# One transfer for r and k, routing in pairs of chunks, and another order in a batch's last chunk: an RWKV-attention and mixture-of-experts kernel on one core

## The chip, the cores and the metric

The kernel runs on one NeuronCore of a Trainium2 chip. The metric is device time in microseconds of one execution, as the median of three runs. The engines are named as in the profile: PE (TensorE, matmuls), PEld (its weight loads), DVE (VectorE), ACT (ScalarE), POOL (GpSimd) and SP (SyncE, which here only issues transfers).

## What is computed

Attention comes first: a recurrence with a 48 x 48 state per head, over 4 batches, 8 heads and 768 steps. Its output rows (3072 rows of 384) then go through a mixture of experts with one expert per row:

```
for t in range(S):
    kt, vt, rt = (k[:, :, t], v[:, :, t], r[:, :, t])
    cur = np.einsum('bhd,bhe->bhde', u[None] * kt, vt)
    y[:, :, t] = np.einsum('bhd,bhde->bhe', rt, state + cur)
    state = w[None, :, :, None] * state + np.einsum('bhd,bhe->bhde', kt, vt)
...
logits = x @ w_gate
expert_idx = np.argmax(logits, axis=1)
...
h = np.maximum(np.einsum('ecd,edf->ecf', disp, w1), 0.0)
y = np.einsum('ecf,efd->ecd', h, w2)
...
out[i] = gate_w[i] * y[expert_idx[i], pos[i]]
```

`disp` holds, for each of 8 experts, its rows in order of arrival; `gate_w` is the softmax weight of the chosen expert.

## The kernel before, in words

**Attention.** The 768 steps of a batch are cut into 6 chunks of 128, so the main loop has 24 chunks (`NI`), `i` from 0 to 23; a batch's last chunk is `i % 6 == 5`. Within a chunk the recurrence becomes matmuls. `load` (L474) brings r and k, transposed, into a tile `dm`: 48 features of the even heads on partitions 0 to 47, those of the odd heads on 64 to 111. It does that in two transfers, one for each part; the first six chunks take 64 rows in the first transfer, so that the unused partitions hold something. `load_rows` (L484) brings k and v as rows (`bd`, 128 partitions). SP issues the loads five chunks ahead; six buffers of `dm` and of `bd` rotate.

One turn of the main loop (L618) does these steps, written out in this order, and each engine runs its own part in just this order (the schedule is by hand):

- `scores(i+1)` (L516, PE): r times k within the chunk, into PSUM tile `a`.
- `prep_keys(i+3)` (L505, DVE): multiplies `dm` by powers of the decay, the tile `ft`.
- `product(i+3)` (L488, POOL): r times k elementwise, `P`, for the bonus term.
- `scatters` (L170, POOL): writes finished rows of x into their expert's place in DRAM, one indirect transfer per chunk; one per turn below turn 16, two from there.
- `mix` (L75, PE): one PSUM tile `c` that holds the bonus of chunk i+2 and the expert logits of chunk i-1; `mixed` (L85, ACT) copies it out as `ct`.
- `update(i)` (L529, PE): k times v for the next state; left out in a batch's last chunk.
- `masks(i+1)` (L524, DVE): the masked scores go over the diagonal tile `s`.
- `pull` (L90): PE transposes `ct`, DVE copies the result out as `l` (L93).
- `turn` (L101, PE): four transposes that give chunk i-1's rows of x, `xp`; `keep_rows` (L107, ACT) copies them out later.
- `values1`, `state_of`, `diag` and `values2` (L548, L537, L494, L559): outputs `y` of chunk i from the state and the masked scores, copied to `xs` by ACT (L569).

**Routing.** `GROUPS` (L32) sets how many chunks are routed together. After a group's last chunk, `route` (L124) runs as a generator in three parts: six DVE instructions (best expert, one-hot `oh`, L127 to L140); then an exponential on ACT, the matmuls that count ranks (`rk`, L145 to L148) and the lane sums on POOL (L151), one per chunk; then six more DVE instructions (slot and 1/sum, L159 to L165). The first part runs at the end of the turn that follows the group's last chunk, the second and third in the turn after that.

**Expert weights.** Expert 0's weights are loaded and split into a high and a low half during the attention turns 3 to 23 (`wstream`, L235: ACT casts at L249, DVE subtractions at L250). `xtrans(0, j)` (L286) transposes the first 160 rows of expert 0 in three pieces `tp0_0` to `tp0_2`, and its `split` makes `xh` (ACT, L295) and `xl` (DVE, L296) of each. After the loop come `layer1(0, f)` (L300) for expert 0, the routing of the last chunks, and then all experts in passes of PE-bound matmuls (L308 to L310, L327 to L329).

**Start.** `setup1` (L382) computes the powers of the decay in `ft`, by squaring the decay six times and multiplying, each squaring followed by a product with the block before; then a reciprocal (L395) and the product (L396) that fills the other half.

Of the kernel before, what the change touches and what calls it, by code (L numbers as in the profile page):

```python
# [6 lines left out]
F32 = mybir.dt.float32  # L7
# [24 lines left out]
GROUPS = [(0, 4), (4, 4), (8, 4), (12, 4), (16, 2), (18, 2), (20, 2), (22, 1), (23, 1)]  # L32


def rwkv_moe(nc, tc, dmj, rkv, bdc, wv, wu, uv, wg, w1, w2, out, cap):
# [4 lines left out]
    with ExitStack() as ctx:  # L40
# [175 lines left out]
        with ExitStack() as mc:  # L216
# [69 lines left out]
            def xtrans(k, j):  # L286
                q, m = PASSES[k][2], PASSES[k][4]
                pool, tag, bufs = ((ps1, "a1", 1) if k else (psA, "a0", 2), (ps1, "u", 1), (psA, "a0", 2) if k < 2 else (ps1, "a1", 1))[j]
# [93 lines left out]
            def setup1():  # L382
                wc = sup.tile([128, NP], F32, name="wc")
                nc.vector.tensor_scalar(out=wc, in0=wp, scalar1=0.6, scalar2=1.22, op0=ALU.max, op1=ALU.min)
                sq = [wc]
                for i in range(7):
                    t = w128 if i == 6 else sup.tile([128, NP], F32, name=f"sq{i}")
                    nc.vector.tensor_tensor(out=t, in0=sq[-1], in1=sq[-1], op=ALU.mult)
                    sq.append(t)
                    if i < 6:  # L390
                        m = 1 << i
                        nc.vector.tensor_tensor(out=ft[:, :, 64 + m:64 + 2 * m], in0=ft[:, :, 64:64 + m],
                                                in1=sq[i].unsqueeze(2).broadcast_to([128, NP, m]), op=ALU.mult)
                rc = sup.tile([128, NP], F32, name="rc")
                nc.vector.reciprocal(out=rc, in_=sq[6])  # L395
                nc.vector.tensor_tensor(out=ft[:, :, 0:64], in0=ft[:, :, 64:], in1=rc.unsqueeze(2).broadcast_to([128, NP, 64]), op=ALU.mult)  # L396
# [51 lines left out]
            nc.sync.dma_start(out=wup.rearrange("q a p -> q (a p)"), in_=wu)  # L448
# [4 lines left out]
            nc.vector.memset(ft[:, :, 64:65], 1.0)  # L453
# [20 lines left out]
            def load(i):  # L474
# [3 lines left out]
                n = 64 if i < 6 else D  # L478
                rows = dmj[b, c].rearrange("h d m -> (h d) m")
                nc.sync.dma_start(out=dm[0:n].rearrange("q a p c -> q (a p c)"), in_=rows[0:n])  # L480
                (nc.scalar if i < 2 else nc.sync).dma_start(out=dm[64:64 + D].rearrange("q a p c -> q (a p c)"), in_=rows[D:])
# [98 lines left out]

            load(0)
            nc.scalar.copy(out=wd[:, 0, 0:64], in_=zst)
# [35 lines left out]
            for i in range(NI):  # L618
# [29 lines left out]
                scatters(1 if i < 16 else 2)  # L648
# [3 lines left out]
                each(masks, i + 1)  # L652
                to = place_of(i - 1, sm, rows_of)
# [3 lines left out]
                xp = turn(i - 1, T[i - 1]["xs"], ps1)  # L657
# [3 lines left out]
                if i == NI - 1:  # L661
                    pa.close()
                    psA = mc.enter_context(tc.tile_pool(name="psA", bufs=2, space=PSUM))
# [25 lines left out]
            xtrans(0, 2)()  # L689
# [258 lines left out]
def _layout(r, k, v, w, u, w_gate, w1, w2):  # L948
# [8 lines left out]
    def feats(a, fill):  # L957
# [9 lines left out]
        "dmj": np.stack([rt, kt], 4).reshape(B, NC, 2, D, 2 * NP * C),  # L967
# [25 lines left out]
```

## Time and profile before

| | us |
|---|---|
| median of 3 runs | 397.38 (396.44 to 399.8) |
| the profiled execution, its own time | 397.02 |
| its span, first to last instruction | 395.3 |
| mean granted PE clock over the span | 0.991 of full |

How to read it: the profiled execution took 397.02 us, of which 395.3 are the span of its instructions; the 1.7 us around the span don't depend on what is changed here. The attention loop fills the first 133 us, the passes of the experts the rest. Rows of a timeline give a start, a duration, an engine, a source line, an operation, what is written and read with shapes, how many instructions were merged, and in brackets how long the engine stood idle before them and what ended that.

### The profile page before, as it was taken

How to read it: one execution, taken by the hardware profiler on the slowest of the kernel's cores; microseconds unless marked ns; L12 is line 12 of the kernel's file. 1: busy time of each engine (PE TensorE's matmuls, PEld its weight loads, DVE VectorE, ACT ScalarE, POOL GpSimd, SP SyncE). 2: the span in 40 equal slices, each digit the busy share in tenths (PEclk: the TensorE clock that was granted, in tenths of full speed). 3: DMA queues.
4: the chain of work that ended last, by engine and by line, in shares of the span. 5: the costliest groups of instructions: out<-in, count | busy, mean ns of one | idle time of the engine just before them, and what ended most of it. 6: DMA issues, size and time to landing. Idle time of an engine off the chain costs nothing.

```text
span 395.3 us, 9463 instructions
## 1 busy us (share of the span) xinstructions
PE 375.1 (95%) x3587; PEld 338.4 (86%) x3590; DVE 237.2 (60%) x574; ACT 204.4 (52%) x556; POOL 137.7 (35%) x199
## 2 busy tenths in 40 slices
PE   7999999999989789799999999999999999999993
PEld 3677778777767589799999999999999999999992
DVE  6897889898887466554645645645645645643210
ACT  3668787888578334534624624624624624722301
POOL 6122538585673426601501601601601601201203
PEclk9999999999999899999999999999999999999998
DMA  8999878888722546641634644644644644400102
GB/s 174 260 241 263 219 218 236 259 238 264 200 82 71 175 132 189 203 124 21 209 109 131 177 129 133 176 133 133 183 131 127 185 135 129 144 4 16 44 1 70
DMA packets 20633, 59.93 MB, mean 152 GB/s; under 512 B 4303, under 2 KB 4451, under 8 KB 20577
## 3 DMA queue, kind: packets, MB, share of 16 engines
q1 hardware_dynamic: 14848, 44.12, 40.6%
q0 software_dynamic: 5600, 14.72, 11.5%
q8 instruction: 30, 0.49, 0.6%
q10 hardware_dynamic: 128, 0.39, 0.4%
q14 instruction: 27, 0.21, 0.2%
HBM read 49.98 MB, written 10.03 MB: 152 GB/s over the span
## 4 chain that ended last, share of the span: by engine, by line
PE 74%; issue 12%; ACT 5%; DVE 3%; POOL 2%; DMA 1%; POOLq 1%; another core or an unknown queue 0%; SPq 0%; ACTq 0%; DVEq 0%
PE a L310 8%; PE a L309 8%; PE a L308 8%; PE b L327 7%; PE b L328 7%; PE b L329 7%; PE y L565 6%; PE a L522 6%; PE y L556 3%; PE xp L104 3%; PE c L92 2%; ACT s L503 2%; PE c L82 2%; PE tp L291 2%; PE u L534 2%
## 5 line engine op out<-in xcount | busy, mean ns | idle before, releaser
L335 POOL DMA_INDIRECT out<-yo,ids x32 | 32.3, 1009 | 168.1 <-ACT yo L334 166.2
L308 PE MATMUL a<-xh,ws 128*128 128x416 f32 (+1 forms) x216 | 75.3, 349 | 2.2 <-issue 2.0
L313 ACT ACTIVATE hh<-a 128x416 fp32r<-128x416 f32 (+1 forms) x72 | 35.2, 489 | 74.1 <-PE a L310 69.2
L327 PE MATMUL b<-hh,ws 128*128 128x416 f32 (+2 forms) x216 | 73.4, 340 | 0.0
L309 PE MATMUL a<-xl,ws 128*128 128x416 f32 (+1 forms) x216 | 72.5, 336 | 0.1
L310 PE MATMUL a<-xh,ws 128*128 128x416 f32 (+1 forms) x216 | 72.4, 335 | 0.0
L328 PE MATMUL b<-hl,ws 128*128 128x416 f32 (+2 forms) x216 | 71.7, 332 | 0.3 <-issue 0.3
L329 PE MATMUL b<-hh,ws 128*128 128x416 f32 (+2 forms) x216 | 71.5, 331 | 0.0
L314 DVE SCALAR_TENSOR_TENSOR hl<-a,hh 128x416 fp32r<-128x416 f32 (+1 forms) x72 | 39.8, 553 | 50.8 <-ACT hh L313 38.7
L250 DVE TENSOR_TENSOR ws<-wr,ws 128x384 fp32r<-128x384 f32 (+1 forms) x112 | 67.6, 618 | 2.3 <-ACT ws L249 2.3
L503 ACT ACTIVATE s<-eye,l 128x128 f32<-128x128 f32 x168 | 53.8, 392 | 17.2 <-DVE l L93 16.2
L249 ACT CAST ws<-wr 128x384 fp32r<-128x384 f32 (+1 forms) x112 | 60.0, 558 | 2.2 <-DMA xsd<-xr,slot 2.2
L330 DVE COPY yt<-b 128x416 f32<-128x416 f32 (+2 forms) x27 | 14.6, 542 | 66.7 <-PE b L329 64.3
L492 POOL TENSOR_TENSOR P<-dm 112x512 f32<-112x512 f32 x21 | 27.5, 1312 | 48.7 <-DVE dm L508 20.2
L308 PEld LDWEIGHTS a<-xh,ws 128*128 128x128 f32 x216 | 40.7, 188 | 3.3 <-issue 2.4
L328 PEld LDWEIGHTS b<-hl,ws 128*128 128x128 f32 x216 | 40.8, 189 | 0.8 <-issue 0.5
L309 PEld LDWEIGHTS a<-xl,ws 128*128 128x128 f32 x216 | 40.7, 188 | 0.8 <-DVE xl L296 0.5
L329 PEld LDWEIGHTS b<-hh,ws 128*128 128x128 f32 x216 | 40.6, 188 | 0.4
L327 PEld LDWEIGHTS b<-hh,ws 128*128 128x128 f32 x216 | 40.8, 189 | 0.2
L310 PEld LDWEIGHTS a<-xh,ws 128*128 128x128 f32 x216 | 40.6, 188 | 0.4
L274 POOL DMA_INDIRECT xg<-xsd,pidx x32 | 35.0, 1093 | 15.1 <-issue 7.0
L295 ACT CAST xh<-tp 128x416 fp32r<-128x416 f32 (+1 forms) x27 | 12.6, 480 | 52.3 <-PE tp L291 52.3
(147 smaller groups left out, 569.8 us busy)
## 6 DMA issues: line engine op xcount, KB each, us to landing
wr<-w SPq DMA_DIRECT2D x24, 512.0 KB
wr<-w SPq DMA_DIRECT2D x32, 384.0 KB
bd<-bdc SPq DMA_DIRECT2D x24, 384.0 KB
dm<-dmj SPq DMA_DIRECT2D x40, 192.0 KB
dm<-dmj SPq DMA_DIRECT2D x6, 256.0 KB
xg<-xsd,pidx POOLq DMA_INDIRECT x32
out<-yo,ids POOLq DMA_INDIRECT x32
dm<-dmj ACTq DMA_DIRECT2D x2, 192.0 KB
```

The source lines that it names most:

```text
L249: nc.scalar.copy(out=hi, in_=r)
L250: low.append(lambda: nc.vector.tensor_tensor(out=lo, in0=r, in1=hi.bitcast(F32), op=ALU.subtract))
L274: nc.gpsimd.indirect_dma_start(out=xg[k % 2][:q, i].bitcast(I32), out_offset=None, in_=xsd[:, :], in_offset=bass.IndirectOffsetOnAxis(ap=p ...
L308: nc.tensor.matmul(a, lhsT=wh, rhs=xh[:, d, :n], start=d == 0, stop=False)
L309: nc.tensor.matmul(a, lhsT=wh, rhs=xl[:, d, :n], start=False, stop=False)
L310: nc.tensor.matmul(a, lhsT=wl, rhs=xh[:, d, :n], start=False, stop=d == 2)
L313: nc.scalar.activation(hh[:, f, :n], a, AF.Relu)
L314: nc.vector.scalar_tensor_tensor(out=hl[:, f, :n], in0=a, scalar=0.0, in1=hh[:, f, :n].bitcast(F32), op0=ALU.max, op1=ALU.subtract)
L327: nc.tensor.matmul(o, lhsT=wh, rhs=hh[:, f, :n], start=f == 0, stop=False)
L328: nc.tensor.matmul(o, lhsT=wh, rhs=hl[:, f, :n], start=False, stop=False)
L329: nc.tensor.matmul(o, lhsT=wl, rhs=hh[:, f, :n], start=False, stop=f == 7)
L503: nc.scalar.mul(out=s[:, h, p], in_=eye, mul=bon)
```

## The change

Four edits, made together:

1. `dmj` is padded on the host to 128 rows per chunk, and `load` fetches both halves by one transfer to all 128 partitions (512 KB in place of 192 + 192 KB; in the first six chunks in place of 256 + 192 KB). Chunk 0's is SP's first transfer; the small load of the decay, `wup`, goes to ACT's queue.
2. `setup1` builds the powers by doubling inside one tile `pw`, without the separate squarings; ACT copies the result into the one half of `ft`.
3. `GROUPS` are eleven pairs and two single chunks, in place of four groups of four, three pairs and two singles. `scatters` takes one chunk in every turn.
4. In a batch's last chunk `turn` stands ahead of `pull`. In the loop's last turn, all three `xtrans(0, j)` stand ahead of both, and all three splits are issued together; before, two stood behind them and the third behind the loop.

```diff
-GROUPS = [(0, 4), (4, 4), (8, 4), (12, 4), (16, 2), (18, 2), (20, 2), (22, 1), (23, 1)]
+GROUPS = [(i, 2) for i in range(0, 22, 2)] + [(22, 1), (23, 1)]
...
             def setup1():
-                wc = sup.tile([128, NP], F32, name="wc")
+                pw = sup.tile([128, NP, 65], F32, name="pw")
+                wc = pw[:, :, 1]
+                nc.vector.memset(pw[:, :, 0:1], 1.0)
                 nc.vector.tensor_scalar(out=wc, in0=wp, scalar1=0.6, scalar2=1.22, op0=ALU.max, op1=ALU.min)
-                sq = [wc]
-                for i in range(7):
-                    t = w128 if i == 6 else sup.tile([128, NP], F32, name=f"sq{i}")
-                    nc.vector.tensor_tensor(out=t, in0=sq[-1], in1=sq[-1], op=ALU.mult)
...
+                for m in (1, 2, 4, 8, 16, 32):
+                    nc.vector.tensor_tensor(out=pw[:, :, m + 1:2 * m + 1], in0=pw[:, :, 1:m + 1],
+                                            in1=pw[:, :, m:m + 1].broadcast_to([128, NP, m]), op=ALU.mult)
                 rc = sup.tile([128, NP], F32, name="rc")
...
+                nc.scalar.copy(out=ft[:, :, 64:], in_=pw[:, :, 0:64])
+                nc.vector.reciprocal(out=rc, in_=pw[:, :, 64])
...
-            nc.sync.dma_start(out=wup.rearrange("q a p -> q (a p)"), in_=wu)
+            nc.scalar.dma_start(out=wup.rearrange("q a p -> q (a p)"), in_=wu)
+            nc.sync.dma_start(out=dmb[0].rearrange("q a p c -> q (a p c)"), in_=dmj[0, 0])
...
-                nc.sync.dma_start(out=dm[0:n].rearrange("q a p c -> q (a p c)"), in_=rows[0:n])
-                (nc.scalar if i < 2 else nc.sync).dma_start(out=dm[64:64 + D].rearrange("q a p c -> q (a p c)"), in_=rows[D:])
+                if i:
+                    nc.sync.dma_start(out=dm.rearrange("q a p c -> q (a p c)"), in_=dmj[b, c])
...
-                scatters(1 if i < 16 else 2)
+                scatters(1)
...
                 each(masks, i + 1)
+                if i == NI - 1:
+                    pa.close()
+                    psA = mc.enter_context(tc.tile_pool(name="psA", bufs=2, space=PSUM))
+                    acts = [xtrans(0, j) for j in range(3)]
+                if i % NC == NC - 1:
+                    xp = turn(i - 1, T[i - 1]["xs"], ps1)
                 to = place_of(i - 1, sm, rows_of)
                 pull(c, ct, to)
...
-                xp = turn(i - 1, T[i - 1]["xs"], ps1)
+                if i % NC < NC - 1:
+                    xp = turn(i - 1, T[i - 1]["xs"], ps1)
...
                 if i == NI - 1:
...
-                    acts = [xtrans(0, j) for j in range(2)]
                     take(0)
-                    acts[0]()
-                    acts[1]()
+                    for f in acts:
+                        f()
...
-            xtrans(0, 2)()
```

The edits change what stands where on the engines. On PE, turn 5 (a batch's last chunk), between the mix of chunk 4's `xs` and the values of chunk 5, this stands before:

```order
L82 MATMUL c<-xs_747,wgz 32x128
L92 MATMUL c<-pick,ct 128x16
L104 MATMUL xp_795<-idn,xs_747 128x128 x4
L145 LDWEIGHTS tri
L145 MATMUL rk_801<-oh_760,tri 128x32
```

and this now:

```order
L82 MATMUL c<-xs_757,wgz 32x128
L104 MATMUL xp_804<-idn,xs_757 128x128 x4
L92 MATMUL c<-pick,ct 128x16
L145 LDWEIGHTS tri
L145 MATMUL rk_813<-oh_770,tri 128x16
```

The four transposes of `turn` (L104) stand ahead of the transpose of `pull` (L92), which is the one that waits for ACT's `ct`; the rank matmul behind it covers two chunks (16 columns) in place of four.

On PE in the loop's last turn, from the mix of chunk 22's `xs` to the values of chunk 23, this stands before:

```order
L82 MATMUL c<-xs_2374,wgz 32x128 x4
L92 MATMUL c<-pick,ct 128x16
L104 MATMUL xp_2399<-idn,xs_2374 128x128 x4
L145 LDWEIGHTS tri
...
L148 MATMUL rk_2405<-lane,ones 128x16
L291 MATMUL tp_0_2418<-idn,xg_101 128x128 x2
L291 MATMUL tp_1_2421<-idn,xg_101 128x128 x2
L556 MATMUL y_0_2432<-dm_119,snb_126 64x128 x2
```

and this now (L552 is the line of `values1` in the changed file):

```order
L82 MATMUL c<-xs_2432,wgz 32x128 x4
L291 MATMUL tp_0_2461<-idn,xg_101 128x128 x2
L291 MATMUL tp_1_2464<-idn,xg_101 128x128 x2
L291 MATMUL tp_2_2467<-idn,xg_101 128x128 x2
L104 MATMUL xp_2470<-idn,xs_2432 128x128 x4
L92 MATMUL c<-pick,ct 128x16
L145 LDWEIGHTS tri
...
L148 MATMUL rk_2479<-lane,ones 128x16
L552 MATMUL y_0_2498<-dm_119,snb_126 64x128 x2
```

Ten transposes (six of `xtrans`, four of `turn`) now stand between the mix and the instruction that waits for `ct`, where none stood.

On DVE in turns 2 and 3 (L508, now L504, is `prep_keys`; L544, now L540, the state), this stands before:

```order
L544 SCALAR_TENSOR_TENSOR snb_126<-snb_127,w_137,u 128x48 x4
L508 TENSOR_TENSOR dm_114<-dm_114,ft 112x1024
L526 COPY_PREDICATED s_121<-msk,a_597 128x1024
L93 COPY l_464<-c 128x16
L544 SCALAR_TENSOR_TENSOR snb_127<-snb_126,w_137,u 128x48 x4
L508 TENSOR_TENSOR dm_115<-dm_115,ft 112x1024
```

and this now:

```order
L540 SCALAR_TENSOR_TENSOR snb_126<-snb_127,w_137,u 128x48 x4
L127 TENSOR_REDUCE mx_574<-l_446 128x2
...
L140 TENSOR_TENSOR z_583<-l_446,mx_574 128x16
L504 TENSOR_TENSOR dm_114<-dm_114,ft 112x1024
L522 COPY_PREDICATED s_121<-msk,a_588 128x1024
L93 COPY l_620<-c 128x16
L540 SCALAR_TENSOR_TENSOR snb_127<-snb_126,w_137,u 128x48 x4
L159 TENSOR_TENSOR ps_672<-rk_629,oh_581 128x16
...
L165 RECIPROCAL xr_123<-zs_676 128x2
L504 TENSOR_TENSOR dm_115<-dm_115,ft 112x1024
```

Six instructions of routing stand in each of the two turns where none stood; with pairs, every turn from 2 on carries six.

## Rows read from the trace of the kernel before

**Rows 1.** The page, part 1: busy time, share and instructions by engine.

```profile
PE 375.1 (95%) x3587; PEld 338.4 (86%) x3590; DVE 237.2 (60%) x574; ACT 204.4 (52%) x556; POOL 137.7 (35%) x199
```

**Rows 2.** Busy time by stage: turns 2-5, 6-11, 12-17, 18-22, 23.

```profile
core 0: us, PE busy (x) PEld busy (x) DVE busy (x) ACT busy (x) POOL busy (x), PEclk, DMA share, GB/s
27.56:46.85 19.29, 18.79 (x337) 15.00 (x340) 16.58 (x42) 14.92 (x51) 7.22 (x10) 1.00 0.99 248
46.85:76.08 29.23, 27.98 (x510) 22.35 (x511) 25.21 (x56) 23.43 (x78) 18.96 (x18) 1.00 0.78 231
76.08:105.36 29.28, 28.73 (x515) 22.96 (x517) 27.09 (x66) 23.33 (x79) 18.00 (x21) 1.00 0.86 250
105.36:132.73 27.37, 23.96 (x400) 18.48 (x402) 19.58 (x71) 18.94 (x64) 15.13 (x19) 1.00 0.32 105
132.73:137.86 5.13, 5.04 (x48) 3.79 (x51) 2.87 (x17) 1.92 (x7) 2.16 (x3) 0.69 0.45 142
```

**Rows 3.** Timeline of DVE at the start: decay arrives, `ft`, first and sixth chunk.

```profile
4.07 0.17 DVE L384 TENSOR_SCALAR wc<-wup 128x4 f32<-128x4 f32 x1 [2.34 <-DMA wup<-wu]
...
6.03 0.42 DVE L396 TENSOR_TENSOR ft<-ft,rc 128x256 f32<-128x256 f32 x1
...
6.73 1.23 DVE L508 TENSOR_TENSOR dm<-dm,ft 112x1024 f32<-112x1024 f32 x1 [0.27 <-DMA dm<-dmj]
...
25.46 1.22 DVE L508 TENSOR_TENSOR dm<-dm,ft 112x1024 f32<-112x1024 f32 x1 [0.80 <-DMA dm<-dmj]
```

**Rows 4.** Transfers in two short stretches (columns as in rows 2).

```profile
3.00:7.00 4.00, 4.00 (x12) 1.50 (x11) 2.60 (x17) 0.97 (x4) 2.58 (x42) 1.00 1.05 191
...
61.00:62.00 1.00, 1.00 (x26) 0.79 (x25) 1.00 (x3) 0.30 (x1) 0.85 (x1) 1.00 1.02 390
```

**Rows 5.** Timeline of DVE: third part of `route`, four chunks, then two.

```profile
63.02 0.18 DVE L159 TENSOR_TENSOR ps<-rk,oh 128x32 f32<-128x32 f32 x1
...
64.06 1.22 DVE L508 TENSOR_TENSOR dm<-dm,ft 112x1024 f32<-112x1024 f32 x1
...
112.68 0.16 DVE L159 TENSOR_TENSOR ps<-rk,oh 128x16 f32<-128x16 f32 x1
...
113.66 1.22 DVE L508 TENSOR_TENSOR dm<-dm,ft 112x1024 f32<-112x1024 f32 x1
```

**Rows 6.** Timeline of PE in turn 5.

```profile
40.27 0.42 PE L82 MATMUL c<-xs,wgz 128*32 128x128 f32 x8
41.19 0.40 PE L92 MATMUL c<-pick,ct 128*128 128x16 f32 x2 [0.50 <-ACT ct L87]
41.43 0.64 PE L104 MATMUL xp<-idn,xs 128*128 128x128 f32 x4
...
42.71 1.08 PE L565 MATMUL y<-s,bd 128*48 128x128 f32 x16
```

**Rows 7.** Timeline of POOL and ACT in turns 18 and 19.

```profile
107.21 0.98 POOL L172 DMA_INDIRECT xsd<-xr,slot  x1 [0.30 <-issue]
...
108.69 0.65 ACT L569 COPY xs<-y 128x256 f32<-128x256 f32 x2 [1.28 <-PE a L522]
...
113.23 0.98 POOL L172 DMA_INDIRECT xsd<-xr,slot  x1 [0.30 <-issue]
...
114.72 0.68 ACT L569 COPY xs<-y 128x256 f32<-128x256 f32 x2 [1.27 <-PE a L522]
```

**Rows 8.** PE around turn 23 (timeline), the stage's clock (windows), six transposes (chain).

```profile
131.26 0.39 PE L92 MATMUL c<-pick,ct 128*128 128x16 f32 x2 [1.73 <-ACT ct L87]
...
133.73 1.95 PE L565 MATMUL y<-s,bd 128*48 128x128 f32 x16
...
137.58 0.28 PE L310 MATMUL a<-xh,ws 128*128 128x256 f32 x1
...
133.00:135.00 2.00, 2.00 (x28) 1.65 (x22) 1.79 (x11) 0.16 (x1) 0.00 (x0) 0.50 0.74 209
...
157.90 0.65 PE tp L291 x6
```

More of the change, by code (lines that the diff above doesn't have):

```diff
@@ L287, in xtrans @@
                 q, m = PASSES[k][2], PASSES[k][4]
-                pool, tag, bufs = ((ps1, "a1", 1) if k else (psA, "a0", 2), (ps1, "u", 1), (psA, "a0", 2) if k < 2 else (ps1, "a1", 1))[j]
+                pool, tag, bufs = ((ps1, "a1", 1) if k else (psA, "a0", 2), (ps1, "u", 1) if k else (psA, "a0", 2), ((ps1, "u", 1), (psA, "a0", 2), (ps1, "a1", 1))[min(k, 2)])[j]
                 tp = pool.tile([128, m * q], F32, tag=tag, name=f"tp{k}_{j}", bufs=bufs)
@@ L382, in setup1 @@
             def setup1():
-                wc = sup.tile([128, NP], F32, name="wc")
+                pw = sup.tile([128, NP, 65], F32, name="pw")
+                wc = pw[:, :, 1]
+                nc.vector.memset(pw[:, :, 0:1], 1.0)
                 nc.vector.tensor_scalar(out=wc, in0=wp, scalar1=0.6, scalar2=1.22, op0=ALU.max, op1=ALU.min)
-                sq = [wc]
-                for i in range(7):
-                    t = w128 if i == 6 else sup.tile([128, NP], F32, name=f"sq{i}")
-                    nc.vector.tensor_tensor(out=t, in0=sq[-1], in1=sq[-1], op=ALU.mult)
[L389 to L393, printed above, removed]
+                for m in (1, 2, 4, 8, 16, 32):
+                    nc.vector.tensor_tensor(out=pw[:, :, m + 1:2 * m + 1], in0=pw[:, :, 1:m + 1],
+                                            in1=pw[:, :, m:m + 1].broadcast_to([128, NP, m]), op=ALU.mult)
                 rc = sup.tile([128, NP], F32, name="rc")
-                nc.vector.reciprocal(out=rc, in_=sq[6])
-                nc.vector.tensor_tensor(out=ft[:, :, 0:64], in0=ft[:, :, 64:], in1=rc.unsqueeze(2).broadcast_to([128, NP, 64]), op=ALU.mult)
+                nc.scalar.copy(out=ft[:, :, 64:], in_=pw[:, :, 0:64])
+                nc.vector.reciprocal(out=rc, in_=pw[:, :, 64])
+                nc.vector.tensor_tensor(out=ft[:, :, 0:64], in0=pw[:, :, 0:64], in1=rc.unsqueeze(2).broadcast_to([128, NP, 64]), op=ALU.mult)
+                nc.vector.tensor_tensor(out=w128, in0=pw[:, :, 64], in1=pw[:, :, 64], op=ALU.mult)
                 return wc
@@ L579, in each @@
                     f(i, *a)
+            nc.scalar.copy(out=wd[:, 0, 0:64], in_=zst)
             load(0)
-            nc.scalar.copy(out=wd[:, 0, 0:64], in_=zst)
             load(1)
@@ L661, in rwkv_moe @@
                 if i == NI - 1:
-                    pa.close()
-                    psA = mc.enter_context(tc.tile_pool(name="psA", bufs=2, space=PSUM))
-                    acts = [xtrans(0, j) for j in range(2)]
                     take(0)
-                    acts[0]()
-                    acts[1]()
+                    for f in acts:
+                        f()
                 state_of(i)
@@ L966, in _layout @@
     arrays = {
-        "dmj": np.stack([rt, kt], 4).reshape(B, NC, 2, D, 2 * NP * C),
+        "dmj": np.pad(np.stack([rt, kt], 4), [(0, 0)] * 3 + [(0, 64 - D)] + [(0, 0)] * 3).reshape(B, NC, 128, 2 * NP * C),
         "rkv": np.stack([rows(r), rows(k), rows(v)], 3),
```

3 lines of the change are left out of this document (removed).

## The prediction

> **What bounds the kernel now.** I read the page's busy shares first [rows 1]: PE is busy 95% of the span, DVE 60%, ACT 52%. Such an average hides stages, so the table by stage comes next [rows 2]. The passes of the experts, from 138 us to the end, are PE's and the change leaves them alone; what it can win or lose lies before. From turn 2 on PE is busy nearly throughout: 18.79 of 19.29 us, 27.98 of 29.23, 28.73 of 29.28. But DVE stands close behind it: 16.58, 25.21 and 27.09 us of the same stretches. In turns 18 to 22 neither is full (PE 23.96 and DVE 19.58 of 27.37 us): something there waits. The timeline then shows three kinds of wait: DVE for transfers at the start [rows 3], PE for ACT's `ct` in a batch's last chunk [rows 6] and, much longer, in turn 23 [rows 8], and ACT for PE in turns 18 and 19 [rows 7].
>
> **The start.** DVE gets the decay at 4.07 us, starts the product that fills `ft` at 6.03 and the first chunk's keys at 6.73, the last 0.27 of it waiting for the chunk [rows 3]. From 4.07 to 6.03 stand fifteen instructions in 1.96 us; the new chain has eight up to the same product. The removed squarings ran in between the products, though, while in the new chain each product waits for the one before. Bounds: nothing, or the seven instructions at the mean step of 0.13 us, 0.9 us. I take 0.3, nearer to nothing, since the new chain is all dependent. The copy on ACT lies beside the reciprocal and the product on DVE. The 0.27 us go only if the chunk comes in earlier as well: it is now SP's first transfer, alone but for the small `wup`.
>
> **The loads.** In the stretch 3 to 7 us, when nearly only halves of `dm` move, the 16 transfer engines are busy throughout (share 1.05) and bring 191 GB/s; at 61 to 62 us, with `bd` and weights to 128 partitions, they bring 390 GB/s at the same share [rows 4]. So a chunk's 448 KB cost about 2.4 us of transfer time now (estimated, 0.459 MB by 191) and the 512 KB some 1.35 (0.524 MB by 390). If the new load ran no faster than the mix does in turns 2 to 5, at 248 GB/s and full share [rows 2], it would cost 2.1: from six loads a gain of 1.8 us, and 0.13 MB more in each chunk from then on. Either way chunk 5's wait of 0.80 us at 25.46 [rows 3] should go: -0.8. Nothing after it waits on a load, so the remaining time is not won.
>
> Which of the two rates holds for the new load no row settles, since no r and k goes to 128 partitions there. The Trainium skill (SBUF — State Buffer, Door 1: The DMA port swizzle) says that partitions 0 to 63 reach only eight of the sixteen ports, that two transfers to the two halves hardly add up, and that one to all 128 reaches them all; it gives 196 and 328 GB/s at 1 MiB. The trace agrees in kind, with 191 against 390 GB/s. By the page's figures the load would fall from 2.3 to 1.6 us (an estimate from them), and this term would stay -0.8; by the rate of the mix it could come to nothing (rival 3).
>
> **Routing in pairs.** Each half of a `route` takes about the same on DVE whether it covers four chunks or two: the third part 63.02 to 64.06 us, 1.04, and 112.68 to 113.66, 0.98 [rows 5]. Eight pairs in place of four groups of four make 16 halves at 1.0 in place of 8 at 1.04: +7.7 us on DVE, all of it in turns 2 to 17: four halves for two in turns 2 to 5 (+2), six for two in turns 6 to 11 (+4), six for four in turns 12 to 17 (+1.8). Added to DVE's busy time [rows 2]: 18.6 of 19.29, 29.2 of 29.23, 28.9 of 29.28. So it just fits, and DVE becomes the bound of turns 6 to 17; what stands in a batch's last chunk can't be won there. Bounds: 0 if all fits in DVE's gaps, +7.7 if all lands on the path. DVE's gaps sum to 8.9 us over these stages, so I stay near the lower end: +0.6 in turns 2 to 5 (where the wait for chunk 5, just removed, was one of the gaps), +0.5 in 6 to 11, 0 in 12 to 17. Queued behind the six instructions on DVE is `prep_keys`, which is used two turns later, then `masks` and the copy `l`, for which ACT's diagonals wait; ACT has that slack only while DVE is not late by a whole turn.
>
> **Turn ahead of pull.** In turn 5 PE ends the mix at 40.69 and starts `pull` at 41.19: 0.50 us idle [rows 6]. The four transposes of `turn` (0.64 us, the last of it beside what follows) now fill this gap. -0.5 in turn 5; in turns 11 and 17 DVE is the bound by the sum above, and I count 0 and -0.3.
>
> **Turns 18 and 19.** ACT is idle 1.28 and 1.27 us before it copies `y`, though PE's matmuls for it are over; both end 0.50 us after the second of two scatters in a row ends on POOL (108.19 to 108.69, 114.21 to 114.72) [rows 7]. With one scatter per turn no second one stands there. Whether that is the cause the trace doesn't show: bounds 0 and -2.6. I take the middle, -1.3, since two cases are too few to tell.
>
> **Turn 23.** The mix ends at 129.53; PE then waits 1.73 us for `ct` [rows 8], and after `pull`, `turn`, the ranks and four transposes starts the values shortly before 132.73 [rows 2]. By then its granted clock has fallen from 2.4 to 1.2 GHz (0.50 in 133 to 135 us), so the second half of the values takes 1.95 us in place of 1.08 [rows 8, 6]. The first nine matmuls of `layer1` end at 137.86, with waits for the third split in between. In the new order: 0.65 for six transposes [rows 8] and about 0.5 for `turn` lie in the wait; `pull` (0.39) and the ranks take it from 131.26 to 131.75; the values, 2.95 us from 132.73 to 135.68 now, take some 1.65 by the ratio of 1.08 to 1.95, to 133.4; nine matmuls of `layer1`, at about 0.11 each like the transposes, and some waiting for three splits that now stand together on ACT and DVE, to 135. That is -2.8. If the clock falls all the same, the values and `layer1` cost what they did and only the moved transposes are won: -1.4. If `ct` comes as soon as PE is through, -3.4. I take -2.8: PE now idles 0.6 us there, not 1.73. All behind this point, the routing of the last chunks and through it the first splits of expert 1, moves along with it.
>
> **The sum**, against the profiled execution: -0.3 - 0.8 + 0.6 - 0.5 + 0.5 - 0.3 - 1.3 - 2.8 = -4.9. 397.02 - 4.9 = 392.1 us; the median of the runs lies 0.36 above the profiled one, so 392.5.
>
> **The rivals.**
>
> 1. DVE becomes a real bound (slower). Place: turns 2 to 17, where pairs put six instructions into every turn. Price: all 7.7 us on the path in place of 0.6, with the two gains of turns 5 and 17 lost: -4.9 + 7.1 + 0.8 = +3.0, 400.4 us. It decides once DVE's queue has no idle time left between `snb` and the next `masks`. For it speaks that my sums fill turns 6 to 11 to 29.2 of 29.23 us; against it, that DVE has 8.9 us of gaps in total in turns 2 to 17 and most of what it makes is needed a turn or more later.
> 2. The waits are only moved. The stall of turns 18 and 19 isn't the scatters', and the clock falls in turn 23: -4.9 + 1.3 + 1.4 = -2.2, 395.2 us. For it: no row ties PE to POOL. Against it: the idle time of PE in turn 23 shrinks to a third.
> 3. The load gets no cheaper per byte (the edit doesn't do what it says). At 248 GB/s it still gains 1.8 us over six loads, then adds 0.13 MB per chunk to engines that are busy 0.78 to 0.99 [rows 2]; a chunk then comes late somewhere in turns 5 to 8, and the 0.8 is lost again: 393.3 us. By itself this hardly shows.
> 4. Everything goes: both stalls (-2.6), no cost in turns 2 to 11, `ct` at once in turn 23: -4.9 - 1.3 - 1.1 - 0.6 = -7.9, 389.5 us.
>
> **How the numbers follow.** Forecast 392.5 us, chance 0.47 with rival 3 in it (it lies 0.8 us away); rival 2 has 0.28, rival 4 has 0.13, rival 1 has 0.12. A run of this kernel tells about 1% (3.97 us) from no change: below 393.4 counts as faster, above 401.4 as slower. The forecast's own spread is about 391 to 394, of which some three quarters lie below 393.4: 0.36 and 0.13 from rival 4, and a little of rival 2, give 0.51 for faster. Somewhat under half of rival 1 lies above 401.4: 0.05 for slower. The rest, 0.44, is the same. The range reaches up past rival 2 to the lower part of rival 1 and down to rival 4: 389.5 to 397.5.
>
> **What would show each step.** The start: first keys at about 6.4 us, no wait for a transfer before chunk 5's. The loads: over 300 GB/s in the first 7 us. Routing: DVE busy about 29 us in turns 6 to 11, these turns no longer than 30. Turn 5: no idle PE between L82 and L92. Turns 18 and 19: about 1.3 us shorter each if the scatters were to blame. Turn 23: granted clock 1.00 and the first `layer1` over within 6 us of the mix. I would be wrong in kind if turns 6 to 17 together took over 61 us, or if turn 23 were shorter and the passes of the experts started no earlier.

## The result, and the profile after

On the chip of the first comparison the changed kernel takes 392.9 us (median of 20 runs) and the kernel before 397.4 (20 runs): ratio 0.9898, 95% interval 0.9869 to 0.9927. The forecast was 392.5. Several of the terms behind it came out very differently from the working, and on another chip the change gains nothing (ratio 1.0002 in e5 below). Both facts have the same two causes, which the experiments look for.

The profiled execution took 391.79 us, its span 390.1 (before 397.02 and 395.3). Where the 5.2 us went, stage by stage, counted from the first matmul of `values1` in a turn (0.07 us ahead of the bounds of [rows 2]; a turn's length below is from that point to the next turn's); the last column is worked out from e9 and e5 below, the two kernels on chips where the time before is 387.7 us:

| stage | forecast | first chip | chips of e9, e5 |
|---|---|---|---|
| to turn 2 | -0.3 | +0.36 | +0.48 |
| turns 2 to 5 | -0.7 | -0.93 | -0.44 |
| turns 6 to 11 | +0.5 | +0.52 | +1.32 |
| turns 12 to 17 | -0.3 | +0.68 | +1.12 |
| turn 18 to the end of the mix in turn 23 | -1.3 | +0.19 | -0.06 |
| from there to the end of the first `layer1` | -2.8 | -3.94 | -1.35 |
| the rest | 0 | -2.04 | -0.54 |
| sum | -4.9 | -5.16 | +0.53 |

Busy time and stages of the changed kernel, which answer to [rows 1] and [rows 2]; the last two windows answer to [rows 8] (the clock in turn 23) and [rows 4] (the loads at the start):

```profile
PE 372.8 (96%) x3591; PEld 336.7 (86%) x3594; DVE 243.0 (62%) x616; ACT 204.7 (52%) x565; POOL 138.0 (35%) x199
```

```profile
27.85:46.21 18.36, 18.32 (x336) 14.70 (x335) 17.12 (x52) 14.74 (x52) 9.34 (x11) 1.00 0.80 265
46.21:75.96 29.75, 28.65 (x510) 22.91 (x509) 28.57 (x80) 23.55 (x81) 17.32 (x19) 1.00 0.79 265
75.96:105.92 29.96, 29.61 (x510) 23.08 (x509) 28.66 (x81) 23.52 (x81) 18.20 (x20) 1.00 0.76 251
105.92:131.72 25.80, 23.57 (x399) 18.56 (x398) 18.44 (x66) 19.23 (x66) 12.34 (x17) 1.00 0.33 111
131.72:134.74 3.02, 3.02 (x49) 2.46 (x49) 2.88 (x13) 1.46 (x6) 0.00 (x0) 1.00 0.39 110
133.00:135.00 2.00, 2.00 (x25) 1.43 (x21) 1.86 (x11) 1.12 (x4) 0.00 (x0) 1.00 0.69 211
3.00:7.00 4.00, 4.00 (x13) 1.53 (x12) 1.99 (x10) 0.41 (x1) 1.96 (x33) 1.00 1.03 401
```

The loads run at 401 GB/s where they ran at 191, the clock in turn 23 is 1.00 where it was 0.50, DVE's busy time in turns 6 to 11 has grown by 3.36 us (25.21 to 28.57). The timeline of DVE at the start and at the sixth chunk's keys, against [rows 3]:

```profile
4.73 0.17 DVE L386 TENSOR_SCALAR pw<-wup 128x4 f32<-128x4 f32 x1 [2.99 <-DMA wup<-wu]
...
6.57 0.42 DVE L393 TENSOR_TENSOR ft<-pw,rc 128x256 f32<-128x256 f32 x1
...
7.09 1.22 DVE L504 TENSOR_TENSOR dm<-dm,ft 112x1024 f32<-112x1024 f32 x1
...
24.94 1.22 DVE L504 TENSOR_TENSOR dm<-dm,ft 112x1024 f32<-112x1024 f32 x1
```

From the decay to the product the new chain takes 1.84 us (4.73 to 6.57) where the old one took 1.96, but the decay itself comes 0.66 us later. The wait for chunk 5 is gone. PE in turn 5, against [rows 6]: no idle time stands before L92 any more.

```profile
40.19 0.42 PE L82 MATMUL c<-xs,wgz 128*32 128x128 f32 x8
40.55 0.66 PE L104 MATMUL xp<-idn,xs 128*128 128x128 f32 x4
41.11 0.40 PE L92 MATMUL c<-pick,ct 128*128 128x16 f32 x2
```

In turn 9 a routing instruction that took 0.17 us elsewhere, and in turn 9 of the kernel before, takes 1.47. POOL's zero fill of `xg` starts with it and ends with it; in turn 13 the same pair stands at 82.22 and 82.24. The timeline of POOL and DVE, beside [rows 5]:

```profile
62.22 0.49 POOL L151 TENSOR_TENSOR lane<-lane,oh 128x8 bf16<-128x8 bf16 x2
...
62.64 1.47 DVE L164 TENSOR_SCALAR zs<-zs 128x2 f32<-128x2 f32 x1
62.65 1.43 POOL L687 MEMSET xg<- 128x1600 f32 x1
```

The waits of ACT in turns 18 and 19 [rows 7] are gone, and three others stand where two indirect transfers still follow each other on POOL: the scatters in turn 20, the gather in turn 21, the scatters of turns 22 and 23. Here is the second transfer of each with the copy that waited; each copy starts 0.53 to 0.68 us after the transfer's end:

```profile
116.92 0.97 POOL L172 DMA_INDIRECT xsd<-xr,slot  x1 [0.30 <-issue]
...
118.42 0.65 ACT L565 COPY xs<-y 128x256 f32<-128x256 f32 x2 [1.29 <-PE a L518]
...
122.24 1.00 POOL L274 DMA_INDIRECT xg<-xsd,pidx  x1 [0.30 <-DVE snb L540]
...
123.92 0.65 ACT L565 COPY xs<-y 128x256 f32<-128x256 f32 x2 [0.93 <-PE y L561]
...
127.59 1.00 POOL L172 DMA_INDIRECT xsd<-xr,slot  x1 [0.31 <-issue]
...
129.24 0.65 ACT L565 COPY xs<-y 128x256 f32<-128x256 f32 x2 [2.63 <-PE y L561]
```

PE in turn 23, against [rows 8]: no wait for `ct`, and the second half of the values at 1.08 us in place of 1.95.

```profile
129.66 0.69 PE L82 MATMUL c<-xs,wgz 128*32 128x128 f32 x8 [1.34 <-ACT xs L565]
...
131.43 0.29 PE L92 MATMUL c<-pick,ct 128*128 128x16 f32 x2
...
132.32 1.08 PE L561 MATMUL y<-s,bd 128*48 128x128 f32 x16
```

Behind that, PE waited 2.04 us at one place in the passes of the kernel before, and 0.80 us in two parts (0.61 and 0.19) in the changed one. It waits for `hl`, with which DVE frees a PSUM tile (167.45 + 0.42 us in the kernel before), and `hl` waits for ACT's `hh`. ACT stood idle for 2.76 us before that while gathers followed each other on POOL, though PE had ended all its matmuls at 165.89, 1.14 us before ACT went on. Rows of the timeline of the kernel before:

```profile
166.52 1.07 POOL L274 DMA_INDIRECT xg<-xsd,pidx  x1 [0.30 <-issue]
167.03 0.38 ACT L313 ACTIVATE hh<-a 128x256 fp32r<-128x256 f32 x1 [2.76 <-PE a L310]
...
167.93 0.39 PE L308 MATMUL a<-xh,ws 128*128 128x256 f32 x1 [2.04 <-issue]
```

### The profile page after: what moved, and what is told of

Same layout as the page of the kernel before. It is cut to its first block, busy times and chain, and to the rows that moved or that the text cites. A ratio compares the mean times of both kernels' runs of the same rounds, so it can differ in the third digit from the quotient of the medians.

```text
span 390.1 us, 9456 instructions
## 1 busy us (share of the span) xinstructions
PE 372.8 (96%) x3591; PEld 336.7 (86%) x3594; DVE 243.0 (62%) x616; ACT 204.7 (52%) x565; POOL 138.0 (35%) x199
## 4 chain that ended last, share of the span: by engine, by line
PE 67%; issue 13%; DVE 9%; ACT 6%; POOL 2%; DMA 1%; POOLq 1%; DVEq 0%; ACTq 0%
PE a L310 8%; PE a L308 8%; PE a L309 8%; PE b L327 7%; PE b L328 7%; PE b L329 7%; PE y L561 4%; ACT s L499 4%; PE a L518 3%; PE y L552 2%; PE tp L291 2%; PE xp L104 2%; POOL out L335 2%; PE yp L343 2%; DVE s L522 2%
```

## The experiments

e1 to e4 ran on one chip (the kernel before takes 394.84 us there), e5 to e8 on another (387.75), e9 to e11 on a third (387.72), e12 on a fourth (395.05). Ratios are to the kernel before on the same chip. The changed kernel itself ran only on the chip of the first comparison and on that of e5 to e8, so the times of the other runs have no changed kernel beside them, and their theories are judged by the rows above all. The lengths of turns come from one profile each.

**e1: the third edit undone.**

```diff
-GROUPS = [(i, 2) for i in range(0, 22, 2)] + [(22, 1), (23, 1)]
+GROUPS = [(0, 4), (4, 4), (8, 4), (12, 4), (16, 2), (18, 2), (20, 2), (22, 1), (23, 1)]
...
-                scatters(1)
+                scatters(1 if i < 16 else 2)
```

> The changed kernel with the third edit undone (groups of four again, two scatters per turn from turn 16). Theory A: pairs cost on DVE what the trace after shows (turns 6 to 17 took 59.7 us against 58.5 before), and what pairs win lies in turns 18 and 19, where the second of two scatters in a row on POOL holds up everybody who waits for PE. Then turns 6 to 17 fall to about 58.5 us or less, turns 18 and 19 rise from 4.8 and 4.6 to about 6.1 us each, turns 20 and 21 fall back to 4.9 and 4.5 us, and the time is within 1 us of the changed kernel's, 392 to 393.5 us. Theory B: the stall of turns 18 and 19 comes from something else in the change (loads, order); then both stay below 5 us and the time falls to about 391 us. Theory C: the pairs are free on DVE and win 2.6 us as forecast; then the time rises to about 395.5 us.

Ratio 0.9955 (0.993 to 0.998), 393.1 us. Theory A: turns 18 and 19 take 6.04 and 6.07 us again, turns 6 to 17 58.02 (59.71 in the changed kernel), and the profiled span is 389.7 against 390.1. So pairs win 2.7 us in two turns and lose 1.7 in turns 6 to 17 and 1.6 in turns 20 to 22 (the profiles come from two chips, both with such waits). In turn 18 (timeline) ACT and DVE are let go together, 0.47 and 0.51 us after the end of the second scatter, and both wait for PE, which had finished; L191 reads a matmul that stands ahead of the scores:

```profile
106.23 0.98 POOL L172 DMA_INDIRECT xsd<-xr,slot  x1 [0.30 <-issue]
107.68 0.65 ACT L565 COPY xs<-y 128x256 f32<-128x256 f32 x2 [1.25 <-PE a L518]
107.72 0.16 DVE L191 TENSOR_TENSOR pen<-pos,ct 128x4 f32<-128x4 f32 x1 [1.28 <-PE a L518]
```

**e2: the fourth edit undone.**

```diff
-                if i % NC == NC - 1:
-                    xp = turn(i - 1, T[i - 1]["xs"], ps1)
                 to = place_of(i - 1, sm, rows_of)
                 pull(c, ct, to)
...
-                if i % NC < NC - 1:
-                    xp = turn(i - 1, T[i - 1]["xs"], ps1)
+                xp = turn(i - 1, T[i - 1]["xs"], ps1)
...
-                    acts = [xtrans(0, j) for j in range(3)]
+                    acts = [xtrans(0, j) for j in range(2)]
```

(with the transposes back behind `prep_values`, the third behind the loop, and their PSUM places as before)

> The changed kernel with the fourth edit undone (turn behind pull, transposes of expert 0 where they were). Theory A: this edit carries most of the gain: from the end of the mix in turn 23 to the end of the first layer1 the trace after has 4.46 us where before had 8.33, so about 3.9 us come back, the granted clock falls to 0.50 in turn 23 again, and the time is about 396.5 us. Theory B: the passes of expert 1 wait for weights (2.0 us idle before, 0.8 after), and that wait swallows part of what turn 23 loses: 394 to 395 us. Theory C: the clock stays at 1.00 because the loop before it is arranged otherwise; then some 1.7 us come back, 394.5 us.

Ratio 0.9995 (0.9976 to 1.0015), 394.43 us: of the four runs on this chip the one without any gain. PE waits 1.51 us for `ct` again, but the clock of this stretch stays at 1.00, so theory C's time comes closest; from the mix to the first `layer1` it takes 6.85 us against 4.39 with the edit, 2.46 more. Turn 4, which ends behind `pull` and `turn` of turn 5, takes 4.73 against 4.25: the 0.50 us before L92 are back. Not all of the lost gain need be the edit's: in this profile the first values come 1.46 us later than in the changed kernel (last section), and whether the other executions share that isn't shown. PE's timeline, and a window of the stage (the next, 134 to 137 us, has 1.00 as well):

```profile
131.86 0.40 PE L92 MATMUL c<-pick,ct 128*128 128x16 f32 x2 [1.51 <-ACT ct L87]
```

```profile
131.00:134.00 3.00, 2.14 (x33) 1.79 (x35) 1.71 (x7) 1.43 (x5) 0.43 (x2) 1.00 0.41 149
```

**e3: the first two edits left out** (the kernel before with the diffs of edits 3 and 4 of the change).

> The kernel before with the third and fourth edits alone (two transfers per chunk, old chain of powers). Theory A: the load edit is worth the wait of 0.80 us for chunk 5 and loses 0.36 us at the start, where the decay arrives 0.66 us later: then the first keys start at about 6.7 us, the sixth chunk's wait is back at about 25.5 us, and the time is 0.4 us above the changed kernel's, about 393.3 us. Theory B: with six routing instructions more on DVE in turns 2 to 5 the chunk's wait lies beside them and costs nothing; then the old loads are 0.4 us faster, 392.5 us. Theory C: with pairs the slow loads come late in more turns; then 394.5 us or more.

Ratio 0.9939 (0.9916 to 0.9961), 392.29 us. Theory B: the first keys start at 6.63 us, the sixth chunk's wait is 0.17 us in place of 0.80, with the old loads; turns 2 to 5 take 18.37 us, as in the changed kernel (18.36). DVE's timeline:

```profile
24.74 1.23 DVE L508 TENSOR_TENSOR dm<-dm,ft 112x1024 f32<-112x1024 f32 x1 [0.17 <-DMA dm<-dmj]
```

**e4: the decay first.**

```diff
-            nc.scalar.dma_start(out=wup.rearrange("q a p -> q (a p)"), in_=wu)
+            nc.sync.dma_start(out=wup.rearrange("q a p -> q (a p)"), in_=wu)
```

> The changed kernel with the small load of the decay as SP's first transfer again, ahead of the first chunk. Theory A: the decay came late because a load of 512 KB on another queue was ahead of it; then it arrives at about 4.1 us in place of 4.73, the first keys start at 6.4 to 6.5 us in place of 7.09, and all behind moves by 0.6 us: about 392.3 us. Theory B: what is won at the start is lost at the first wait for a chunk in turns 1 to 5; then the values of turn 6 still start at about 46.2 us and the time stays 392.9 us. Theory C: ACT's queue is what made it late, and the 512 KB load delays it just as much on SP's: no change in the start of the first keys.

Ratio 0.9919 (0.9895 to 0.9943), 391.34 us. Theory A and more: the decay is there at 2.45 us and the first keys start at 5.39. Then DVE waits 1.49 us for the first bonus, so the first values start 0.74 us earlier than in the changed kernel (12.99 against 13.73), and that is kept up to turn 6 (45.46 against 46.21).

DVE's timeline:

```profile
2.45 0.75 DVE L386 TENSOR_SCALAR pw<-wup 128x4 f32<-128x4 f32 x1 [0.71 <-DMA wup<-wu]
...
5.39 1.23 DVE L504 TENSOR_TENSOR dm<-dm,ft 112x1024 f32<-112x1024 f32 x1
...
9.96 0.17 DVE L93 COPY bon<-c 128x16 f32<-128x16 f32 x1 [1.49 <-PE c L92]
```

**e5: the changed kernel again, on another chip.** No edit.

> The changed kernel itself, unaltered, beside the other runs on this chip, so that they can be compared with it and not only with the kernel before. Every theory expects a ratio to the kernel before of 0.987 to 0.993, as measured first.

Ratio 1.0002 (0.9991 to 1.0013), 387.92 us: outside of what every theory expected. Turns 2 to 17 take what they took in the changed kernel on the first chip (78.09 us against 78.07), but turn 20 takes 4.71 us in place of 5.72, turn 21 4.37 in place of 5.54 and turn 22 4.05 in place of 5.08. The scatters stand on POOL just as they did; the copy of turn 20 starts with the second of them, without waiting:

```profile
117.08 0.98 POOL L172 DMA_INDIRECT xsd<-xr,slot  x1 [0.31 <-issue]
```

```profile
117.19 0.62 ACT L565 COPY xs<-y 128x256 f32<-128x256 f32 x2
```

**e6: the fills of `xg` taken off POOL.**

```diff
-                if i in (9, 13):
-                    nc.gpsimd.memset(xg[i == 13], 0.0)
...
+            for t in xg:
+                nc.scalar.copy(out=t, in_=zst[:, 0:1].unsqueeze(2).broadcast_to([128, 4, XW]))
             c = mix(T[0]["P"], None, ps1)
```

> The changed kernel, with the two zero fills of xg taken off POOL (turns 9 and 13) and done by ACT before the loop. Theory A: in turns 9 and 13 of the trace after a DVE instruction of routing (L164) took 1.47 us in place of 0.17 and ended with POOL's fill, because the fill keeps it from running; with the fills gone it takes 0.17 us both times, turn 10 falls from 5.76 to about 5.0 us, turns 14 and 15 from 5.41 and 5.39 to about 5.0 each, and the time by 1.5 us to some 0.985 of the kernel before. Theory B: DVE is the bound in those turns by its own sum of instructions; then L164 is shorter but turns 10, 14 and 15 stay above 5.3 us and the time is the changed kernel's.

Ratio 0.9999 (0.9988 to 1.0010), 387.75 us. The mechanism is theory A's, the time is not: L164 takes 0.17 us, turn 10 falls from 5.80 to 4.49 us, turn 14 from 5.42 to 4.73, turn 15 from 5.36 to 4.87, 2.5 us together; and the fills, put where ACT was needed (2.93 us from 8.71), move the first values from 13.85 to 16.56 us. Timeline of DVE in turn 9:

```profile
65.48 0.17 DVE L164 TENSOR_SCALAR zs<-zs 128x2 f32<-128x2 f32 x1
```

**e7: a fill between two indirect transfers.**

```diff
+            def space():
+                nc.gpsimd.memset(spc, 0.0)
...
                 for i in range(m):
+                    if k == 0 and i:
+                        space()
...
                 each(product, i + 3)
+                if i == NI - 1:
+                    space()
                 scatters(1)
...
+                    space()
                     scatters(NI)
                     gather(0)
```

> The changed kernel, with a fill of 4 KB per partition (some 0.9 us) on POOL between the two indirect transfers that follow each other in turn 20 (scatters), turns 20 to 21 (the gather) and turns 22 to 23 (scatters). Theory A: the second of two indirect transfers in a row holds up those who wait for PE; apart from each other they don't, so ACT's waits before the copy xs in turns 20, 21 and 22 (1.29, 0.93 and about 1.0 us more than the matmuls need) go, these turns fall from 5.72, 5.54 and 5.08 to about 4.7 us each, and the time by 1 to 2.5 us. Theory B: any second transfer within some 3 us of the first does it, whatever stands between; then the waits last until 0.5 us after the end of the second, which is now 0.9 us later, and the turns get longer by up to 0.9 us each. Theory C: the waits have nothing to do with POOL: no change in these turns.

Ratio 1.0013 (1.0003 to 1.0024), 388.28 us, and no answer: on this chip there were no waits to remove. Turns 18 to 22 take 22.58 us against 22.59.

**e8: all scatters in pairs.**

```diff
-                scatters(1)
+                scatters((1 if i > 19 else 2 if i % 2 == 0 else 0))
```

> The changed kernel, with two scatters in a row in every even turn from 4 to 18 and none in the odd ones, in place of one per turn: the same transfers, paired. Theory A: the second of each pair holds up ACT's copy xs until about 0.5 us after its end on POOL, as in turns 18 and 19 of the kernel before; ACT shows a wait of 0.5 to 1.3 us before xs in those eight turns, they get longer by about 1 us each, and the time rises by 4 to 10 us over the changed kernel's. Theory B: the stalls of turns 18 to 22 come from something that only those turns have; then the eight turns stay within 0.2 us each and the time is the changed kernel's.

Ratio 0.9975 (0.9961 to 0.9989), 386.64 us. No pair holds anybody up on this chip either, so it doesn't tell theories A and B apart. It gains by accident: the fills now run 1.5 us ahead of L164 (61.83 against 63.35), which takes 0.17 us in both turns.

**e9: the kernel before, on a chip of the quick kind.** No edit.

> The kernel before, unaltered, for a profile on the chip on which the other two of this call run. The ratio of the change was 0.990 on the first chip and 1.000 on the one of the last four runs, and the profile of the changed kernel there had none of the waits of turns 20 to 22. Theory A: those waits are the chip's; on a chip on which the kernel before takes about 388 us it shows no wait of ACT before xs in turns 18 and 19 beyond the matmuls, these take about 4.7 us each in place of 6.1, the wait for ct in turn 23 is about 0.5 us in place of 1.73, and no idle PE before expert 1's weights; on one on which it takes 394 us or more they are all there. Theory B: the waits are there on every chip in the kernel before, and its time differs by something else.

387.61 us. Theory A, in every number: turns 18 and 19 take 4.81 and 4.65 us, the wait for `ct` in turn 23 is 0.43 us, the clock in the windows from 126.66 to 130.63 is 1.00, and PE's wait of 2.04 us in the passes is gone. So is the wait of 0.80 us for chunk 5, with the old loads. Timelines of POOL and ACT in turn 18, beside [rows 7], of PE in turn 23, beside [rows 8], and of DVE at the sixth chunk, beside [rows 3]:

```profile
105.50 0.99 POOL L172 DMA_INDIRECT xsd<-xr,slot  x1 [0.30 <-issue]
```

```profile
105.62 0.61 ACT L569 COPY xs<-y 128x256 f32<-128x256 f32 x2
```

```profile
125.30 0.39 PE L92 MATMUL c<-pick,ct 128*128 128x16 f32 x2 [0.43 <-ACT ct L87]
```

```profile
24.78 1.23 DVE L508 TENSOR_TENSOR dm<-dm,ft 112x1024 f32<-112x1024 f32 x1
```

The two profiles of this kernel show one thing more. In turn 6 a single scatter runs, and on the first chip it holds ACT up as well: the copy `ct` starts 0.54 us after the matmul that it reads has ended (L82, 49.73 + 0.42), in e9 0.19 us after it (49.24 + 0.42, with the scatter at 49.54). The turn takes 5.03 us there and 4.67 here. Timelines of the kernel before and of e9:

```profile
50.02 1.00 POOL L172 DMA_INDIRECT xsd<-xr,slot  x1 [0.17 <-ACT xr L111]
...
50.69 0.27 ACT L87 COPY ct<-c 128x128 f32<-128x128 f32 x1 [0.73 <-PE u L534]
```

```profile
49.85 0.27 ACT L87 COPY ct<-c 128x128 f32<-128x128 f32 x1 [0.37 <-PE c L82]
```

**e10 and e11: a better version, without and with the fills between transfers.** On top of e4 (e11 adds the lines of e7):

```diff
-                if i in (9, 13):
-                    nc.gpsimd.memset(xg[i == 13], 0.0)
...
                 ct = mixed(c, wk)
+                for t in {1: (xg[0],), 2: (xg[1][:, 0:2],), 3: (xg[1][:, 2:4],)}.get(i, ()):
+                    nc.scalar.copy(out=t, in_=zst[:, 0:1].unsqueeze(2).broadcast_to([128, t.shape[1], XW]))
                 update(i)
```

> The changed kernel with the decay loaded first, and with the zero fills of xg done by ACT in turns 1, 2 and 3, where it waits 2.38, 0.87 and 0.75 us for DVE's l. Theory A: both gains add up, 0.75 us at the start and some 2.5 us in turns 10, 14 and 15, while the fills (1.47 us in all for each xg) lie in ACT's waits: about 3 us less than the changed kernel, 384.8 us on a chip like the last, 389 on one like the first. Theory B: the fills on ACT delay the diagonals in turns 1 to 3, and what is won later is lost there: 1 us or less is left.

> The same with a fill of some 0.9 us on POOL between the indirect transfers that follow each other in turns 20 to 23. Theory A: on a chip where the second of two in a row holds up those who wait for PE it takes 1 to 3 us off the kernel of the run beside it; on one where it doesn't, it changes nothing (within 0.5 us). Theory B: the time between them doesn't matter, and where the waits are there they get longer by the 0.9 us of the fill.

Ratios 0.991 (0.989 to 0.993), 384.03 us, and 0.9906 (0.9887 to 0.9926), 384.04 us. e10 is theory A; e11 came onto a chip without the waits, where both of its theories expect no change. In e10 turns 6 to 17 take 57.21 us, where the kernel before takes 57.29 on the same chip (e9): without the fills, routing in pairs costs no more there than the fourth edit wins. ACT's timeline in turn 1 shows that the fill lies in the wait for `l`, of which 0.97 us are left:

```profile
19.57 1.53 ACT L648 COPY xg<-zst 128x1600 f32<-128x1600 f32 x1
22.06 1.86 ACT L499 ACTIVATE s<-eye,l 128x128 f32<-128x128 f32 x6 [0.97 <-DVE l L93]
```

**e12: spaced and unspaced pairs in one kernel** (e11 without the fill between the scatters of turn 20).

```diff
-                    space()
                     scatters(NI)
                     gather(0)
```

> The kernel of the last run with the fill left out between the two scatters of turn 20 and kept between the two parts of the gather and between the scatters of turns 22 and 23: spaced and unspaced pairs in one profile. On a chip that shows the waits at all (the kernel before at 394 us or more), theory A: ACT waits about 1.3 us before xs in turn 20 (the unspaced pair) and, beyond the matmuls, not at all in turns 21 and 22 (the spaced ones): turns 21 and 22 stay at about 4.4 to 4.7 us, turn 20 takes 5.7. Theory B (the time between doesn't matter): turns 21 and 22 are longer as well, by 1 us or more. On a chip without the waits both theories expect about 0.991 of the kernel before and no wait in any of these turns, and nothing is told apart.

This run came onto a chip with the waits (before 395.05 us). Ratio 0.9794 (0.9731 to 0.9857), 386.33 us (4 runs). Theory A: turn 20 takes 5.66 us, turns 21 and 22 4.49 and 4.05. The timeline of POOL and ACT shows both cases. The copy of turn 20 starts 0.47 us after the end of the second, unspaced scatter (113.06 + 0.97). In turn 21 the second gather runs from 118.61 to 119.62, `y` is ready at 118.87 (L567, 117.79 + 1.08), and the copy starts at 119.00, in the middle of it:

```profile
113.06 0.97 POOL L173 DMA_INDIRECT xsd<-xr,slot  x1 [0.30 <-issue]
114.50 0.65 ACT L571 COPY xs<-y 128x256 f32<-128x256 f32 x2 [1.23 <-PE a L524]
...
117.47 0.96 POOL L273 MEMSET spc<- 128x1024 f32 x1
118.61 1.01 POOL L280 DMA_INDIRECT xg<-xsd,pidx  x1 [0.17 <-issue]
119.00 0.61 ACT L571 COPY xs<-y 128x256 f32<-128x256 f32 x2
```

Turn 21 by itself proves little, since an unspaced pair of gathers doesn't always hold anybody up: in turn 21 of the kernel before, on the first chip, the copy also starts in the second gather (and so in e2, at 124.74 in the one from 124.62):

```profile
124.06 1.01 POOL L274 DMA_INDIRECT xg<-xsd,pidx  x1 [0.30 <-DVE slot L161]
124.17 0.61 ACT L569 COPY xs<-y 128x256 f32<-128x256 f32 x2
```

Turn 22 says more. Its pair of scatters is spaced here and it takes 4.05 us, as on the chips without waits; with the same groups and order and no fill between, on chips with waits, it takes 5.00 to 5.08 us (the changed kernel, e3, e4). That is one execution, and whether the time between the two or the fill itself does it wasn't separated.

The interval lies below that of the changed kernel on the first chip (0.9869 to 0.9927), though not on the same chip. e11, the same kernel but for one line, is at 0.9906 on a chip without waits, where the changed kernel (on another such chip) has 1.0002. So this version beats the kernel before on a chip of either kind; that it beats the changed one is seen only across chips.

## Why the prediction was right, and where not

**The sum** was right (392.5 against 392.9) for this chip, and half of its terms were wrong. The errors cancel, so that it came so close is luck. The range held for it, but no rival spoke of the chip: on the one of e5 no gain came at all.

**The start** (-0.3): the sign failed. The step "the 0.27 us go only if the chunk comes in earlier as well" asked for the chunk, while what came later was the decay, moved to ACT's queue beside a load of 512 KB. I had costed its move at nothing. The chain itself won 0.12 us (1.84 against 1.96), not 0.3. e4 has the decay early again, and its first values start 0.74 us earlier than the changed kernel's.

**The loads** (-0.8): the rate was right and its worth was not. They run at 401 GB/s, above the 300 named, and the wait is gone; but with the old loads it is 0.17 us in e3 and nothing in e9. So 0.80 was the value of one profile, and the faster loads win nothing there. Rival 3 was wrong on the rate and right that the load edit hardly shows. The Trainium skill (SBUF — State Buffer, "Can I just issue two DMAs to hit both halves?") says that only one transfer across all 128 partitions reaches all ports; 191 and 401 GB/s at a share of 1.05 and 1.03 agree. The rate is above the 328 GB/s that the Trainium skill (SBUF — State Buffer, Door 1: The DMA port swizzle) gives for 128 partitions at 1 MiB.

**Routing in pairs** (+0.6, +0.5, 0): turns 6 to 17 cost 1.2 us more on the first chip, where the prediction looked for a cost in DVE's instructions of routing. e6 and e10 show another mechanism: with the fills gone, the instructions cost no more than the fourth edit wins (57.21 against 57.29 us), and the collision of L164 with POOL's fill costs 2.5. It shows as 1.2 on the first chip because the kernel before is slower there itself: 58.51 us, and 57.29 in e9, where the changed kernel takes 59.7 on either kind of chip. Pairs bring it about since POOL then adds two lanes (0.49 us) and not four ahead of the fill, which starts with L164 and not 1.54 us behind it (65.29 and 63.75 in the kernel before). The step that failed is "so it just fits, and DVE becomes the bound": it fits, and an instruction that takes 1.47 us in place of 0.17 was in no sum. The edit moves work on POOL, and I had costed it on DVE alone. The Trainium skill (SBUF — State Buffer, Who interferes with whom) has the rule: DVE and GpSimd share a pair of SBUF ports; a `tensor_scalar` can run in a mode that takes it, and whoever has it keeps the other out for its whole instruction. That L164 ended 0.03 us behind the fill (64.11 and 64.08) agrees; in which mode it ran, and which of the two had the ports first (they start at 62.64 and 62.65), no row shows.

**Turn ahead of pull** (-0.5, 0, -0.3): right for turn 5, and nearly for the others. Turn 4, which ends behind them, takes 4.25 us in place of 4.79. At the batch ends of turns 11 and 17 what is won in turns 10 and 16 (e10: 4.47 and 4.26 us, where e9 has 4.84 and 4.79) is given back in the next turn (5.02 and 5.50, where e9 has 4.67 and 5.07): ACT waits there 1.1 and 1.4 us for DVE's `l`.

**Turns 18 and 19** (-1.3, bounds 0 and -2.6): the scatters were to blame, and the full 2.73 us came, above the bound. But the step forgot the pairs that remain: turns 20 to 22 and the mix in turn 23 got 2.9 us longer, and the stage as a whole 0.19. e12 speaks for two transfers close to each other as the cause; the kernel before in turn 6 shows that one alone can do it too, for less time. That it doesn't happen on every chip e5 and e9 show.

**Turn 23** (-2.8): right in mechanism, too small, -3.94. The clock held, `ct` came while PE was busy, and the first `layer1` was over 4.39 us after the mix (within 6). The term that was sized too small is the wait before `pull`: from the end of the mix to `pull` 1.08 us passed (130.35 to 131.43), where the working left the 1.73 as they were. On a chip without the waits it is worth 1.35 (5.76 to 4.41): the wait of 1.73 us that the clock fell with was itself such a wait. The second scatter of its pair ended 0.53 us ahead of `ct`.

**The rest** (0): "all behind this point moves along with it" failed, by 2.04 us. Some 1.2 of it is PE's wait for `hl` in the passes, 2.04 us against 0.80, and behind that stands ACT, held up while gathers follow each other on POOL. In e9 ACT waits at most 0.28 us beside the same gathers, so this is again the wait that the chip decides. It comes and goes between profiles (0.2 us in e1, 2.1 in e3); why stays open, as do the other 0.8 us.

**Rivals.** Rival 2 (the waits are only moved) had the outcome of turns 18 to 22 right, though the scatters were to blame after all, and turn 23 wrong. Rival 1 is what remains in turns 6 to 17 on the chips of e9 and e5, +2.4 us, by a mechanism it didn't name. Its price has a slip: routing stands in the sum with 1.1 us, not 0.6, so all 7.7 on the path come to +2.5, and 399.9 us in place of 400.4.

## What to carry to other kernels

When an edit shortens work on POOL, look at what then runs beside what on DVE: two fills of 1.43 us cost 2.5 here through an instruction of 0.17. Where an engine waits for PE, try a distance between two indirect transfers, or other work, and try it on a chip that shows such waits. Before you price a wait from one profile, ask whether another execution or another chip shows it.

## What was not expected of the hardware

- Indirect transfers on POOL kept ACT and DVE from going on with what PE had finished, on the three chips where the kernel before takes 394.84 to 397.4 us; on the two others (387.7 us) never. Of two in a row the second did so in most cases until 0.45 to 0.70 us after its end; in turn 21 of the kernel before, of e1 and of e2 the copy went on in the middle of it, and in turn 6 of the kernel before a single scatter delayed `ct`. A fill of 0.96 us between the two was enough in the one run that could show it (e12). What holds the signal back, when it lets go and why only there, stays open; whether the chips differ in anything else wasn't tried.
- The clock at the start. In e2 and e7 the granted clock fell in the first turn (0.64 and 0.73 from 12 to 16 us), behind 1.90 and 1.86 us of idle PE before the first scores, and the first values came 1.2 to 1.5 us later than in the changed kernel on the first chip (15.19 and 14.94 against 13.73). In e6, with ACT's fills there, it fell too; in the eleven other profiles PE idled there between nothing and 1.14 us, and the clock held. In e4 and what is built on it, where the decay comes first, PE didn't idle. PE and the window in e7:

```profile
8.37 1.16 PE L524 MATMUL a<-dm 48*128 48x128 f32 x16 [1.86 <-DVE dm L510]
```

```profile
12.00:16.00 4.00, 4.00 (x41) 1.90 (x42) 2.66 (x4) 1.74 (x6) 0.00 (x0) 0.73 1.03 402
```
